# Attention and a long convolution on one core: early jobs in single PSUM banks, sums inverted as 128 rows of 32, and other due times for queries and output projection

## The chip, the core and the metric

The kernel runs on one core of one Trainium2 chip. The core has five engines with queues of their own: PE (matrix products, with PEld for its weight loads), DVE (vector), ACT (scalar functions), POOL, and SP, which here issues nearly all transfers. [...] PE writes its results to PSUM, which has eight banks of 512 fp32 columns on 128 partitions; DVE and ACT empty them to SBUF. The metric is the device time of one execution in microseconds.

## The reference

Two independent parts are computed and laid side by side along the last axis: attention with 32 query heads that share one key head and one value head of 16 columns, and a gated long convolution.

```python
q = (x @ wq).reshape(B, S, H, Dh).transpose(0, 2, 1, 3)      # S 2048, D 512, H 32, Dh 16
k, v = x @ wk, x @ wv
p = softmax(einsum("bhqd,bkd->bhqk", q, k) * Dh ** -0.5)
a = einsum("bhqk,bkd->bhqd", p, v).transpose(0, 2, 1, 3).reshape(B, S, H * Dh) @ wo
...
k_shift = sum(k_pad[:, t:t + S, :] * shift_k[:, ks - 1 - t] for t in range(4))
kv = k_shift * B_v
y = irfft(rfft(kv, 2 * S) * rfft(ssm_k, 2 * S))[:S] + kv * ssm_D
out = concatenate([a, B_q * y], axis=-1)
```

## The kernel before

**Turns and stacks.** The attention is cut into 16 stacks of 8 heads and 512 queries (`NST = 16`, stack n has token chunk n // 4 and head group n % 4). A stack has 64 turns, the whole 1024. A turn is one score tile of 128 x 1024 in two PSUM banks (`scores`, line 1206: eight products in tiles of 64 rows by 32 columns), one exponential of it on ACT (`exp`, 1227, the operation at line 1229) and half a product with the values (`pv`, 1235, 1259). The row that keeps the exponent in range and the row of ones in `vx`, from which each query's sum comes, go through the same products. The probabilities of the first eight turns are kept (`HELD = 8`), and their products with the values come late in stack 0. Each finished stack is copied out of PSUM (`acc_out`, 1273), written to DRAM (`od`), read again in another layout and divided by its sums (`heads`, 1341): two loads (`r`, the sums copied to the 16 rows of each head, and `o`), a clamp (1350), a reciprocal of 128 x 512 (1352), and three vector operations that make two fp16 halves `oc` of the quotient. The last stack is normalised in SBUF (`over`, 1452) in two halves.

**An order written out ahead.** The program is made by a planner in Python that keeps a clock for each of PE, ACT and DVE (`self.pe`, `self.act`, `self.dv`) and writes every engine's instructions in the order in which its own costs let them come; the chip runs this fixed order, whatever the real times. `attend` (1287) walks the turns. In a turn it writes the scores, then either a product with values or other work for PE, as long as its planned end is within a limit behind the turn's start T, then the exponential, one or two DMA issues, and what DVE has time for. Costs are in `T_EXP, T_SC, T_PV, LAT` and the like (47, 48); a DVE step states its cost with `yield`, as `yield T_REC` (700 ns) ahead of the reciprocal.

**Early jobs.** Before turn 64 the other work is a list of early jobs (`early_jobs`, 915): turning x of later token chunks (`turned`, `x_turn`), their keys and values (`keys`, `own`, `values`), the queries of head group 1, a bound, and two small products. Each writes one of the two halves of a single two-bank tile `F` and has vector steps that empty it. `early_fill` (1043) picks by due time, for as many units of 216 ns as fit within `EARLY_LIM = 480`. `kdone` and `vdone` are the times from which scores and products of a chunk of 512 keys may use it.

**Fill.** Later the other work is a list of jobs (`fill`, 238; the products at line 308), each with a due turn; of those whose inputs are there, the one with the least due turn is taken, one at a time, in the two-bank tile `f`. They are the convolution of two blocks of 256 channels, as transforms by products with tables (`short`, `long`, `backward`, due turns in `DUE`, line 45) with 16-point transforms and products of spectra on DVE between them (`dft16`, `product`), the queries of the remaining groups, two at a time (`q_group`, 1082; `rest_of_q`, 1133), and the output projection (`wo_job`, 1389; `wo_part`, 1396) for four stacks at a time. Line 467 empties a forward transform, 647 a last one, 1094 a query job, 1405, 1418 and 1435 projections.

**What waits for what around the change.** In `rest_of_q` a query group is begun at turn `due - 110` with `due = 256 c + 128 h - 40`, and its job is due 120 turns before `due`. `stacks` (1162) loads a stack's queries about 58 turns ahead. `heads(n)` for n from 4 on waits until the projection of the four stacks before (`("wo", n // 4 - 1)`) is done, as `oc` has four buffers. The projection of stacks 4c to 4c + 3 is due at turn `256 (c + 1) + 150`: 406, 662, 918. At the end, `last` (1473) writes what is left of the jobs, then the second half's `over`, the last product and the last store.

**Prologue.** Chunk 0 is turned, its keys and its group 0 queries are made in tile `acc`, the 512 columns of keys spread to 128 rows in `F[:, 0]` (`rows_mm`), and their maximum is spread by a product into `F[:, 1]` (880), from which the bound's weights `wbz` are made (883). All four transposes of chunk 1 are done here.

## Time and profile before

| | |
|---|---|
| three runs | 1032.59, 1037.88, 1040.52 us; median 1037.88 us |
| the profiled execution | 1034.93 us, of which its span is 1033.2 us |
| granted TensorE clock | 0.990 of full speed |
| first exponential begins, last one ends | 20.66 us, 1008.6 us |
| the costliest lines | exponential 947.9 us (ACT), values 553.1 us and scores 435.0 us (PE, overlapping), 50.3 us of reciprocals (DVE) |
| transfers | 84.86 MB, mean 82 GB/s |

Times in views are microseconds from the span's start. Busy time of an engine is the union of its instructions; matmuls are pipelined, so that a busy PE is not at its peak. Behind a group of instructions stands the idle time of its engine just before them, and what ended it.

### The profile page before, as it was taken

The page shows a single profiled execution, that of the slowest core. Times are in us where ns is not written, and L with a number is a line of the kernel's source. Part 1 is how long each engine was busy: PE and PEld are TensorE (multiplying, and loading weights), DVE is VectorE, ACT ScalarE, POOL GpSimd, SP SyncE. Part 2 cuts the span into 40 slices and gives each one's busy share as a digit, 9 for nine tenths or more (in the row PEclk, how much of TensorE's full clock was granted, in tenths as well). Part 3 has the DMA queues.
Part 4 walks back from the last instruction along what each step waited for, and adds up shares of the span by engine and source line. Part 5 has one row for each costly group of instructions (what it writes and reads, how often), then busy time and mean ns, then how long its engine had stood idle before and what let it go on. Part 6 is the DMA issues. An engine that isn't in the chain of part 4 may idle for free.

```text
span 1033.2 us, 53539 instructions
## 1 busy us (share of the span) xinstructions
PE 947.0 (92%) x24556; PEld 486.1 (47%) x24556; DVE 698.2 (68%) x827; ACT 963.0 (93%) x1035; POOL 42.9 (4%) x106
## 2 busy tenths in 40 slices
PE   7799999998999999889999999999899988889985
PEld 4334444544554554344545555555444433335661
DVE  4324488659963499999954994464949999980303
ACT  4699999999999999999999999999899999989880
POOL 3820000000000000000000000000000000000000
PEclk9899999999999999999999999999999999999997
DMA  6123354232112513101133352433220120103311
GB/s 217 42 97 117 114 154 136 70 115 65 49 54 85 151 24 100 34 27 55 34 110 93 103 151 95 137 101 90 80 81 23 48 55 3 59 5 99 119 35 55
DMA packets 78020, 84.86 MB, mean 82 GB/s; under 512 B 10734, under 2 KB 66392, under 8 KB 77788
## 3 DMA queue, kind: packets, MB, share of 16 engines
q1 hardware_dynamic: 76156, 80.77, 25.9%
q8 instruction: 194, 3.18, 1.3%
q10 hardware_dynamic: 1632, 0.60, 0.2%
q14 instruction: 38, 0.31, 0.1%
HBM read 55.91 MB, written 25.43 MB: 79 GB/s over the span
## 4 chain that ended last, share of the span: by engine, by line
ACT 42%; DVE 25%; PE 23%; issue 10%; DMA 0%; ACTq 0%; POOL 0%; DVEq 0%; POOLq 0%
ACT p L1229 41%; PE a L1259 9%; DVE sp L368 6%; PE s L1222 5%; PE f L308 5%; DVE r L1352 2%; DVE sp L437 2%; DVE u L411 1%; DVE sp L413 1%; DVE sp L415 1%; DVE t L437 1%; DVE sp L467 1%; PE s L720 1%; PE f L851 1%; PE f L727 1%
## 5 line engine op out<-in xcount | busy, mean ns | idle before, releaser
L1229 ACT ACTIVATE p<-s 128x1024 f32<-128x1024 f32 x1016 | 947.9, 1046 | 28.6 <-PE s L1222 25.5
L1259 PE MATMUL a<-p,vx 64*32 64x512 f32 (+1 forms) x8640 | 553.1, 565 | 1.1 <-issue 1.1
L1222 PE MATMUL s<-st,kst 49*32 49x512 f16 x8192 | 435.0, 380 | 47.1 <-ACT p L1229 42.0
L1222 PEld LDWEIGHTS <-kst 49*32 49x32 f16 x8192 | 199.7, 89 | 366.9 <-issue 325.9
L1259 PEld LDWEIGHTS a<-p,vx 64*32 64x32 f32 x8640 | 172.3, 106 | 26.8 <-issue 3.7
L368 DVE TENSOR_TENSOR sp<-sp 128x1024 f32<-128x1024 f32 x96 | 111.0, 1218 | 0.0
L467 DVE COPY sp<-f 128x1024 f32<-128x1024 f32 x32 | 39.1, 1223 | 85.9 <-PE f L308 85.8
L308 PE MATMUL f<-wo,o 64*32 64x512 f16 x1440 | 56.0, 379 | 4.2 <-DVE wp L1418 2.6
L368 DVE TENSOR_TENSOR sp<-sp,sp 128x1024 f32<-128x1024 f32 x48 | 56.2, 1220 | 0.4
L308 PE MATMUL f<-sp,fi 64*32 64x128 f32 (+1 forms) x1472 | 51.4, 312 | 3.1 <-issue 2.6
L308 PE MATMUL f<-xT,wq 64*32 64x512 f16 x1344 | 51.0, 375 | 1.8 <-DVE sp L467 1.6
L1352 DVE RECIPROCAL r<-r 128x512 f32<-128x512 f32 x15 | 50.3, 3353 | 0.5
L1275 DVE COPY ao<-a 128x1024 f32<-128x1024 f32 x15 | 18.4, 1225 | 46.0 <-PE a L1259 45.9
L279 POOL MEMSET tok<- 1x2 f32 x58 | 5.4, 93 | 936.0 <-PE f L308 928.3
L308 PE MATMUL f<-hT,ff 64*32 64x256 f32 (+1 forms) x1376 | 41.2, 321 | 2.1 <-DVE sp L467 1.8
L308 PE MATMUL f<-va,ff 64*32 64x128 f32 (+1 forms) x1504 | 41.6, 308 | 1.1 <-DVE va L555 1.1
L647 DVE TENSOR_TENSOR q<-f,q 128x1024 f32<-128x1024 f32 x8 | 9.8, 1225 | 47.2 <-PE f L308 47.2
L308 PEld LDWEIGHTS f<-sp,fi 64*32 64x32 f32 x1472 | 32.3, 105 | 15.4 <-issue 5.9
L308 PEld LDWEIGHTS f<-va,ff 64*32 64x32 f32 x1504 | 28.2, 106 | 16.0 <-issue 3.4
L552 DVE TENSOR_TENSOR va<-va,t 128x512 f32<-128x512 f32 x48 | 33.2, 691 | 1.4
L550 DVE TENSOR_TENSOR t<-kk 128x512 f32<-128x512 f32 x48 | 33.1, 689 | 1.0
L308 PEld LDWEIGHTS f<-hT,ff 64*32 64x32 f32 x1376 | 26.2, 106 | 15.8 <-issue 3.7
(162 smaller groups left out, 576.1 us busy)
## 6 DMA issues: line engine op xcount, KB each, us to landing
ff<-in_ff SPq DMA_DIRECT2D x64, 128.0 KB
od<-ao SPq DMA_DIRECT2D x30, 256.0 KB
qd<-qp SPq DMA_DIRECT2D x45, 128.0 KB
st<-qd SPq DMA_DIRECT2D x60, 96.0 KB
kk<-in_B_k SPq DMA_DIRECT2D x38, 128.0 KB
va<-in_B_v SPq DMA_DIRECT2D x32, 128.0 KB
hin<-in_B_ssm_k SPq DMA_DIRECT2D x32, 128.0 KB
fi<-in_fi SPq DMA_DIRECT2D x32, 128.0 KB
```

Of the source, the lines that this page charges most:

```text
L308: last = self.nc.tensor.matmul(F[32 * q : 32 * q + 32, rho, cols + a : cols + b], w[rows, 32 * q : 32 * q + 32], x[rows, a:b], start=begin ...
L368: v.tensor_tensor(part(out), part(a), part(b), op)
L411: v.tensor_scalar(u, x, float(np.sin(ang)), None, ALU.mult)
L437: self.nc.vector.tensor_tensor(out, a, b, op)
L467: self.nc.vector.tensor_copy(c[:, :, 2 * m2 : 2 * m2 + 2, :].rearrange("p q m n -> p m q n"), F.rearrange("p m (q n) -> p m q n", q=2))
L550: v.tensor_tensor(tmp, kx(i), tap(i), ALU.mult)
L552: v.tensor_tensor(a, a, tmp, ALU.add)
L1222: self.nc.tensor.matmul(out, self.kst[rows, c0 : c0 + 32], x, start=True, stop=True)
L1229: i = self.nc.scalar.activation(p, self.s, AF.Exp, scale=DH**-0.5 / SC / SC)
L1259: nc.tensor.matmul(out, self.vx[rows, k, :], p, start=i == 0, stop=i == NK - 1)
L1275: self.nc.vector.tensor_copy(a, self.acc)
L1352: nc.vector.reciprocal(r, r)
```

## The change

**Early jobs.** The two-bank tile `F` and its pool are gone in the early stage. A new pool `pb` has two tags of one bank each, and every early job gets a tile of its own in one of them (`one`); the pool of the fill's tile `f` is opened when the first fill job asks for it. Items of early jobs carry planned costs in ns instead of units: a transpose 440, a half of the keys 440, two products of 256 columns for the rows of keys (450 each) instead of four of 128, the values as four items of 230. A job is taken if it is ready within 150 ns, an item if it ends within `EARLY_LIM`, now 1000, of T, with `T_SHAPE` = 220 for the first item of a turn. Ties are broken by the order in the list. The early stage counts as over only when DVE has emptied the last job.

**Prologue.** One transpose of chunk 1 (dk 3) moves to the early jobs, with the split of weight groups 2 and 3 on POOL behind it. The product that spreads the maximum writes `pa[:, 1]`, and two transposes stand before it instead of one. The scaling of one of them goes from ACT to DVE.

**Sums.** For stacks 0 to 13 the sums are loaded as 128 rows of 32 (`rl`), clamped and inverted there, written to DRAM (`rd`) and loaded again, copied 16 times. Arrivals are planned at 8000 and 9000 ns after the issue, by a new argument of `fetch`. Stack 14 keeps the old layout, with the reciprocal cut in four quarters and `T_REC` = 860 for each.

**Due times.** A query group's `due` is 60 turns later for all groups but the first (`+ 20` for `- 40`; the first's is the same), and it is begun up to 500 turns ahead instead of 110. The projection's due turns become 400, 720 and 860.

```diff
-T_REC = 700.0
+T_REC = 860.0
+WO_DUE = (400, 720, 860)
-FILL_LIM, EARLY_LIM, PV_LIM, T_SWAP = 380.0, 480.0, 600.0, 1100.0
+FILL_LIM, EARLY_LIM, PV_LIM, T_SWAP, T_SHAPE = 380.0, 1000.0, 600.0, 1100.0, 220.0
...
+    def one(self, n):
+        return self.pb.tile([P, 512], F32, tag=f"b{n}", name=self.nm("b"))
...
-        c = slice(i * P, i * P + P)
-        self.nc.tensor.matmul(b[:, c], self.msk[:, PROJ], kvs[:, c], start=i == 0, stop=i == 3)
+        c = slice(i * 256, i * 256 + 256)
+        self.nc.tensor.matmul(b[:, c], self.msk[:, PROJ], kvs[:, c], start=i == 0, stop=i == 1)
...
-        self.x_turn(1, 0, acc[:, 0])
-        self.k_max(0, F[:, 0])
-        h16 = self.k_high(0, F[:, 0], nc.scalar)
-        self.k_rows(0, F[:, 0], h16)
-        nc.tensor.matmul(F[:, 1, 0:1], self.msk[:, REP], self.kmx[:, 0:1], start=True, stop=True)
+        self.k_max(0, rows)
+        h16 = self.k_high(0, rows, nc.scalar)
+        self.k_rows(0, rows, h16)
+        self.x_turn(1, 0, pa[:, 0])
+        x1 = self.one(1)
+        self.x_turn(1, 1, x1)
+        nc.tensor.matmul(pa[:, 1, 0:1], self.msk[:, REP], self.kmx[:, 0:1], start=True, stop=True)
...
-    def early_fill(self, units, force=False):
+    def early_fill(self, limit, force=False):
         began = False
-        while units > 0:
-            ready = lambda j: max([s.t for s in j[2]] + [min(b.t for b in self.bank)])
-            new = [j for j in self.early if ready(j) < INF and (force or ready(j) + LAT <= self.pe + (units - 1) * T_UNIT)]
+        end = lambda cost: self.pe + cost + (0.0 if began else T_SHAPE) <= limit
+        while True:
+            ready = lambda j: max([s.t for s in j[2]] + [min(b.t for b in self.bank)]) + LAT
+            new = [j for j in self.early if ready(j) < INF and (force or max(self.pe, ready(j)) - self.pe < 150.0)]
...
-                due = 4 * 64 * c + 128 * h - (40 if c or h else -40)
-                yield lambda now: self.turn >= due - 110
+                due = 256 * c + 128 * h + (20 if c or h else 40)
+                yield lambda now: self.turn >= due - 500
...
-        h = self.fetch([(r, od[DH:32]), (o, od[0:DH])], self.od_h[n], first=True)
-        yield self.at(h)
-        yield 400.0
-        nc.vector.tensor_scalar(r, r, 1e-30, 1 / OS, ALU.max, ALU.mult)
-        yield T_REC
-        nc.vector.reciprocal(r, r)
+        if n < NST - 2:
+            rl = w.tile([P, 32], F32, tag="rl", bufs=2, name=self.nm("rl"))
+            h = self.fetch([(rl, od[DH].rearrange("h (a b) -> h a b", b=32))], self.od_h[n], first=True, arrive=8000.0)
+            h1 = self.fetch([(o, od[0:DH])], self.od_h[n], first=True, arrive=9000.0)
+            yield self.at(h)
+            yield 120.0
+            nc.vector.tensor_scalar(rl, rl, 1e-30, 1 / OS, ALU.max, ALU.mult)
+            yield 300.0
+            nc.vector.reciprocal(rl, rl)
+            rd = self.rd[n].rearrange("(i h) n -> i h n", i=1)
+            h = self.fetch([(self.rd[n].rearrange("h (a b) -> h a b", b=32), rl)], Stamp(self.dv), first=True)
+            h = self.fetch([(r, rd.broadcast_to([DH, 8, 512]))], h, first=True, arrive=9000.0)
+            yield self.at(h, h1)
+        else:
+            h = self.fetch([(r, od[DH:32]), (o, od[0:DH])], self.od_h[n], first=True)
+            yield self.at(h)
+            yield 430.0
+            nc.vector.tensor_scalar(r, r, 1e-30, 1 / OS, ALU.max, ALU.mult)
+            for i in range(4):
+                yield T_REC
+                nc.vector.reciprocal(r[:, i * P : (i + 1) * P], r[:, i * P : (i + 1) * P])
...
-                j = self.wo_job(i, range(4 * c, 4 * c + 4), out, 256 * (c + 1) + 150)
+                j = self.wo_job(i, range(4 * c, 4 * c + 4), out, WO_DUE[c])
```

147 lines of the change are left out of this document (76 added, 71 removed).

## The prediction, made before the changed kernel ran

> **What bounds the kernel now.** I read the page first, then a table of the span cut at its stages, then what ACT and PE waited for, then the DVE and PE order at the places where ACT waited.
>
> ```profile
> span 1033.2 us, 53539 instructions
> PE 947.0 (92%) x24556; PEld 486.1 (47%) x24556; DVE 698.2 (68%) x827; ACT 963.0 (93%) x1035; POOL 42.9 (4%) x106
> L1229 ACT ACTIVATE p<-s 128x1024 f32<-128x1024 f32 x1016 | 947.9, 1046 | 28.6 <-PE s L1222 25.5
> ```
>
> These three lines are of the page: the span, busy time by engine, and the costliest group, with what ended ACT's idle time. The table by stage:
>
> ```profile
> 20.66:45.34 24.68, 18.22 (x241) 9.11 (x234) 9.57 (x22) 15.74 (x16) 23.45 (x24) 0.86 0.15 44
> 45.34:84.00 38.66, 36.93 (x692) 14.90 (x696) 14.98 (x32) 35.23 (x36) 8.39 (x10) 1.00 0.24 78
> 84.00:395.00 311.00, 297.58 (x7868) 151.31 (x7854) 214.09 (x250) 308.88 (x333) 1.88 (x21) 1.00 0.32 93
> 395.00:525.00 130.00, 118.64 (x2924) 57.97 (x2909) 123.46 (x128) 127.23 (x138) 0.62 (x7) 1.00 0.18 53
> 525.00:770.00 245.00, 237.60 (x6776) 127.87 (x6767) 152.59 (x177) 241.87 (x262) 2.42 (x20) 1.00 0.35 103
> 770.00:927.00 157.00, 135.52 (x3224) 60.92 (x3223) 150.04 (x172) 151.62 (x165) 1.49 (x6) 0.99 0.13 38
> 958.50:1008.60 50.10, 45.03 (x1679) 33.42 (x1686) 10.23 (x10) 43.64 (x46) 0.36 (x4) 1.00 0.23 71
> 1008.60:1033.20 24.60, 12.25 (x165) 3.84 (x147) 9.67 (x22) 0.03 (x1) 0.09 (x1) 0.78 0.14 52
> ```
>
> The table's columns are the stretch, its length, then busy time of PE, PEld, DVE, ACT and POOL with counts, and the granted clock. ACT's exponentials, one per turn, set the time: 333 of them in the 311 us from 84 to 395, 0.934 us each, with ACT busy 308.88. PE and DVE count only where they make ACT wait, and that is in four places. First, the early stage: 52 exponentials in 63.3 us, so 63.3 - 52 x 0.934 = 14.8 us too many. Second, the long middle from 84 to 927: ACT idle is 2.1 + 2.8 + 3.1 + 5.4 = 13.4 us, 8.2 of it in the two stretches (395 to 525, 770 to 927) where DVE is busy 95% and PE is not full. Third, the last stack: 46 in 50.1 us, 7.1 us over. Fourth, 24.6 us after the last exponential, in which ACT does nothing.
>
> **The change part by part.** All sums are against this execution: 1034.9 us with what lies around its 1033.2 us span. It is 3 us under the median of the three runs, 1037.9; they reach from 1032.6 to 1040.5.
>
> *Prologue.*
>
> ```profile
> 17.39 0.38 PE L880 MATMUL f<-kmx,msk 128*128 128x1 f32 x2 [1.44 <-DVE kst L789]
> ```
>
> The product that spreads the key maximum waited 1.44 us for a vector instruction that reads the other bank of the same tile; in the new order it writes a tile that this instruction does not read, behind two transposes instead of one. What follows it (the copy kmr, wbz, the products with it, the first scores) comes earlier by at most 1.44 minus the second transpose, about 0.7 us, and by nothing if the copy still stands behind L789 on DVE. One copy goes from ACT to DVE and one transposition into the early jobs; both are behind the first scores. The first 128x512 projection in two products of 256 columns instead of four of 128 streams the same columns: 0. I take -0.7 (0 to -1).
>
> *Early jobs.* Two edits pull against each other.
>
> ```profile
> PE f L768 <- DVE kmx L792: 1.6, 2, 0.8
> PE f L740 <- DVE xc L931: 1.2, 1, 1.2
> PE f L727 <- DVE vx L775: 1.2, 1, 1.2
> PE f L764 <- DVE xf L931: 1.1, 1, 1.1
> ```
>
> The waits of PE are given as total, times and longest. Two rows of the table by stage, and ACT's order, where the bracket is the idle time before:
>
> ```profile
> 30.00:32.60 2.60, 1.67 (x33) 1.05 (x31) 1.71 (x3) 1.84 (x3) 2.43 (x3) 1.00 0.53 154
> 32.60:39.40 6.80, 5.40 (x56) 2.11 (x48) 2.56 (x7) 3.53 (x4) 6.47 (x6) 0.50 0.14 42
> ```
>
> ```profile
> 35.62 1.02 ACT L1229 ACTIVATE p<-s 128x1024 f32<-128x1024 f32 x1 [1.54 <-PE s L1222]
> 37.52 1.02 ACT L1229 ACTIVATE p<-s 128x1024 f32<-128x1024 f32 x1 [0.88 <-PE s L1222]
> 39.65 1.94 ACT L1229 ACTIVATE p<-s 128x1024 f32<-128x1024 f32 x2 [1.10 <-PE s L1222]
> ```
>
> Each wait of PE here (5.1 us in four rows) stands in PE's queue in front of the next scores, and most are for an instruction that empties the other bank. With a tile for each bank, and a rule that a job begins only when it is ready within 150 ns of planned time, most of the 5.1 us goes. The dip of the granted clock to 0.50 from 32.6 to 39.4 adds three gaps, 3.5 us. On the other side, EARLY_LIM goes from 480 to 1000: a job may end 1000 ns after the turn's planned start T, the next scores take 216 and the latency 60, so the next exponential starts at T + 1276 instead of T + 904 at worst, 0.37 us late in each turn with a job. The 22 early jobs of the list, the longer ones spread over several turns, make some 30 turns with a job, so 11 us at worst, less the 220 ns of changing shape for each group that disappears when jobs are put together. So the ends are -11 (waits, dip and half of the changes of shape gone) and +6 (11 lost, 5 won). I take -6, nearer the gain, because PE is busy only 18.22 of 24.68 us in the first stretch, where most of the loss is: there is room to do the same work without making ACT late.
>
> [...]
>
> POOL gets the last two weight splits behind one more split of x. It is busy 23.45 of 24.68 us there, but their reader, the queries of the remaining groups, starts only when the early jobs are over: 0. Those jobs now also count as open until DVE has emptied them: under 1 us, where fill work is plentiful: 0.
>
> *A stack's sums as 128 rows of 32.*
>
> ```profile
> L1352 DVE RECIPROCAL r<-r 128x512 f32<-128x512 f32 x15 | 50.3, 3353 | 0.5
> L1350 DVE TENSOR_SCALAR r<-r 128x512 f32<-128x512 f32 x15 | 6.3, 421 | 16.9 <-DMA r<-od 16.9
> 1018.38 0.18 DVE L1462 TENSOR_SCALAR lr<-lr 128x16 f32<-128x16 f32 x1
> 1018.59 0.26 DVE L1464 RECIPROCAL lr<-lr 128x16 f32<-128x16 f32 x1
> ```
>
> And two places in ACT's order:
>
> ```profile
> 744.58 57.53 ACT L1229 ACTIVATE p<-s 128x1024 f32<-128x1024 f32 x62 [1.56 <-PE s L1222]
> 915.55 1.02 ACT L1229 ACTIVATE p<-s 128x1024 f32<-128x1024 f32 x1 [3.48 <-PE s L1222]
> ```
>
> A reciprocal of 512 columns takes 3353 ns and one of 16 takes 260, so 32 take about 360, and the clamp about 180: 14 stacks save 14 x (3353 + 421 - 540) = 45 us of DVE. The planner booked 700 ns for each reciprocal, so DVE fell 2.65 us behind the written order at every one, and whatever it had to empty next came late to PE, then to ACT. The gaps at 744.58 and 915.55 each follow one or two reciprocals. Stack 14 keeps its way, cut in four quarters of about 840 ns, now booked 860. Each of the 14 stacks issues two more transfers on SP (the inverted rows out, their copies back), 28 in all at 0.55 us; SP is mostly waiting, so 0, unless the load of the copies stands waiting for the store just ahead of it, with the loads of the next scores behind it. DVE also waited 16.9 us for these loads before; the planned arrival goes from 6000 to 8000 and 9000 ns, so less is left. Value in the middle: between -11 (all but the 2 us of the first stretch) and +4 (new waits for the three transfers). I take -6, half of the 13.4 us, as the two stretches with DVE at 95% are where the work goes.
>
> *Queries sooner, output projection moved.* This sets the end.
>
> ```profile
> 656.02 1.23 DVE L1094 TENSOR_SCALAR qp<-f 128x1024 f16<-128x1024 f32 x1 [8.56 <-PE f L308]
> 711.25 1.23 DVE L1405 TENSOR_SCALAR wp<-f 128x1024 f32<-128x1024 f32 x1 [7.24 <-PE f L308]
> 761.36 1.22 DVE L1094 TENSOR_SCALAR qp<-f 128x1024 f16<-128x1024 f32 x1
> 769.99 1.23 DVE L467 COPY sp<-f 128x1024 f32<-128x1024 f32 x1 [5.03 <-PE f L308]
> ```
>
> Those rows are of the time ahead of the second block's transforms. At the end stand:
>
> ```profile
> 1002.60 1.23 DVE L647 TENSOR_TENSOR q<-f,q 128x1024 f32<-128x1024 f32 x1 [13.65 <-PE f L308]
> 1007.88 2.70 PE L1259 MATMUL a<-p,vx 64*32 64x256 f32 x80
> 1008.14 1.23 DVE L1435 SCALAR_TENSOR_TENSOR wp<-f,wp 128x1024 f32<-128x1024 f32 x1 [4.32 <-PE f L308]
> 1017.57 0.77 DVE L1459 STREAM_TRANSPOSE lr<-a 128x256 f32<-128x256 f32 x2
> ```
>
> The second block's convolution waits for its last forward transform, emptied at 769.99. Just ahead of it PE's fill went to two query jobs (656.02, 761.36) and an output projection (711.25), each some 9 to 19 us of the small room that PE has beside scores and values. With the start of the queries 370 turns sooner and their due times 60 turns later, these jobs fall into 395 to 525, where PE is busy 118.64 of 130 us and the convolution waits for DVE; the projection, due at 720 instead of 662, stands behind the forward transforms. Two query jobs and a projection at 10 to 19 us make 30 to 57 us by which 769.99 comes sooner, and three reciprocals fewer take 10 us off the DVE stretch to 927. Against it, three query groups add some 20 us of DVE work to 395 to 525, and the saved reciprocals there give back 10. So the inverse transforms can begin 30 to 45 us sooner, and their last product need not be emptied at 1002.60, in the last stack. Their eight loads and the 24 moved loads of x go with them on SP: 0. What that is worth: of the 7.1 us of the last stack -4 (0 to -7), since the projections of stacks 12 to 14 stay there. In the tail the last values end at 1007.88 + 2.70 = 1010.58, but the final normalisation starts at 1017.57, behind the projection emptied at 1008.14 and one more job: -6.5 (0 to -7).
>
> Sum: -0.7 - 6 - 6 - 4 - 6.5 = -23, so 1012 beside the profiled execution and **1015** beside the median.
>
> **The rivals.**
>
> *The dip stays.* The clock fell after a stretch in which PE was busy 1.67 of 2.60 us, 64%; a new order that leaves PE as idle in the first 20 us brings the dip back, 3.5 us of the early gain are not had, and 1018.5 comes out. Against it: jobs put together leave fewer short idles. [...]
>
> *The gaps are exchanged.* ACT pays 0.37 us in most early turns (+5 instead of -6), and late transfers take the place of late reciprocals in the middle (0 instead of -6); only the end is shorter: 1015 + 17 = 1032. For it: PE is busy 36.93 of 38.66 us from 45 to 84. Against it: the middle gaps follow the reciprocals.
>
> *The chain of stacks is late (slower).* Stacks 8 to 11 are normalised only when the projection of 4 to 7 is done, 12 and 13 only after that of 8 to 11, 14 after 13.
>
> ```profile
> 953.42 0.55 SPq L170 DMA_DIRECT2D r<-od  x1
> 956.79 0.43 DVE L1350 TENSOR_SCALAR r<-r 128x512 f32<-128x512 f32 x1 [4.50 <-DMA r<-od]
> ```
>
> One transfer took 3.4 us here; a stack now has three in a row, 10 us by this row and 23 us by the planner's arrival times (8 + 6 + 9), which decide, as DVE's order follows them. With issue and vector work that is 28 us for each. If the projection of 4 to 7 ends near 765 instead of 711 (due 58 turns later), stacks 8 to 11 are ready at 877, and their projection stands behind the inverse transforms to about 945; then stacks 12 and 13 take 57, stack 14 10 and the last jobs with the tail 35 us: 1047 in the span, 1052 with the rest. It decides from about 930, where before is reached.
>
> *More than the sum.* DVE is nowhere late, and early stage, middle and last stack lose a third of what they lose now: -10 - 9 - 5 - 7 - 0.7 = -32, 1006.
>
> *It does not do what it says.* The order of fill work hardly moves, as every query job waits for x in one buffer, and the banks still wait for each other: only the reciprocals count: 1032.
>
> **How the numbers follow.** A measurement of this kernel tells about 1% from no change, 1027.5 to 1048. Chances: forecast 0.42, dip stays 0.10, more 0.14, gaps exchanged 0.18, does not do it 0.06, chain late 0.10. The likeliest alone runs from 1006 to 1026. Faster takes the forecast, the dip, more and some 0.04 of the exchanged gaps: 0.70. Slower takes 0.06 of the late chain. The same is 0.24. The range goes from 998, below the better case by the prologue's and the middle's bounds, to 1035, above the exchanged gaps; the late chain and a still larger gain are left out.
>
> **What would show it.** Right: 52 early exponentials in under 58 us; no PE wait on DVE across banks; ACT idle under 8 us between 84 and 927; the convolution's last transform emptied before 740 and its last output before 960; the final transpose within 1 us of the last values. Wrong: more 0.3 us gaps before the exponentials of the first 50 turns, DVE waiting for the copies of the inverted rows, or the projection of stacks 8 to 11 emptied after 900.

## The result, and the profile after

| | median | runs | ratio to before, with its 95% interval |
|---|---|---|---|
| before | 1039.2 us | 4 runs, 1032.59 to 1041.31 | 1 |
| changed | 1005.77 us | 4 runs, 1004.52 to 1007.34 | 0.969 [0.9642, 0.9737] |

The changed kernel is 3.1% faster. The forecast was 2.2% (1015 beside a median of 1037.9), and 1005.77 lies in its range of 998 to 1035. The profiled execution of the changed kernel took 1007.34 us. The page of its profile begins:

```profile
span 1005.6 us, 53610 instructions
PE 947.9 (94%) x24556; PEld 483.1 (48%) x24556; DVE 652.6 (65%) x831; ACT 960.8 (96%) x1034; POOL 43.2 (4%) x106
L1244 ACT ACTIVATE p<-s 128x1024 f32<-128x1024 f32 x1016 | 946.1, 1046 | 12.9 <-PE s L1237 8.1
```

The work is the same but for DVE, which has 45.6 us less (652.6 for 698.2). The exponentials are as busy as before (946.1 for 947.9), and the idle time ahead of them has shrunk from 28.6 to 12.9 us. So the gain is waiting, of ACT inside the turns and of everything behind the last turn. The table by stage, with the columns of the earlier one (stretch, length, busy PE, PEld, DVE, ACT, POOL, granted clock, DMA share, GB/s):

```profile
19.24:43.34 24.10, 22.59 (x236) 11.32 (x231) 8.85 (x21) 15.61 (x16) 22.87 (x23) 0.59 0.16 45
43.34:82.00 38.66, 38.53 (x708) 15.76 (x702) 16.86 (x36) 36.03 (x38) 10.27 (x12) 1.00 0.26 85
82.00:395.00 313.00, 304.10 (x8172) 155.46 (x8171) 224.38 (x271) 311.13 (x335) 2.19 (x22) 1.00 0.34 98
395.00:525.00 130.00, 123.93 (x3220) 63.25 (x3205) 109.20 (x122) 128.75 (x139) 1.04 (x10) 1.00 0.26 74
525.00:770.00 245.00, 231.32 (x6244) 116.96 (x6236) 171.97 (x231) 244.41 (x265) 2.08 (x16) 1.00 0.31 91
770.00:927.00 157.00, 144.41 (x3816) 72.64 (x3808) 90.23 (x104) 155.90 (x170) 0.54 (x6) 1.00 0.20 61
929.50:990.00 60.50, 58.22 (x1952) 35.75 (x1951) 17.03 (x24) 59.56 (x65) 1.39 (x7) 1.00 0.13 39
990.00:1005.60 15.60, 6.53 (x80) 2.14 (x64) 4.57 (x11) 0.00 (x0) 0.00 (x0) 0.76 0.11 39
```

From 82 to 927 ACT is idle 1.87 + 1.25 + 0.59 + 1.10 = 4.8 us, where it was idle 13.4 us from 84 to 927. In the stretches 395 to 525 and 770 to 927 DVE was busy 95% and is now busy 84% and 57%. Behind the last exponential lie 15.6 us, where there were 24.6. But the first row shows no gain: 16 exponentials in 24.10 us (24.68 before), now at a granted clock of 0.59 (0.86 before).

The waits of PE (total, times, longest) name no vector instruction that empties the other bank of a shared tile:

```profile
PE s L1237 <- ACT p L1244: 36.1, 106, 0.5
PE s L728 <- DVE lr L1500: 2.9, 1, 2.9
PE s L1237 <- ACT held L1244: 1.4, 2, 0.7
PE f L606 <- DVE sp L475: 1.3, 2, 0.8
PE b L858 <- DVE tok L834: 1.2, 1, 1.2
PE s L900 <- DVE wbz L893: 1.0, 1, 1.0
```

The waits on `p` are the normal pace of the scores. The four rows of waits for `kmx`, `xc`, `vx` and `xf` are gone. The end, in the order of DVE and PE (start, duration, instruction, in brackets the idle time before):

```profile
661.78 0.35 DVE L1369 RECIPROCAL rl<-rl 128x32 f32<-128x32 f32 x1
714.16 1.23 DVE L475 COPY sp<-f 128x1024 f32<-128x1024 f32 x1 [4.68 <-PE f L316]
924.17 1.22 DVE L655 TENSOR_TENSOR q<-f,q 128x1024 f32<-128x1024 f32 x1 [13.00 <-PE f L316]
981.19 1.23 DVE L1475 TENSOR_TENSOR y<-f,wp 128x1024 f32<-128x1024 f32 x1 [13.73 <-PE f L316]
988.40 2.79 PE L1274 MATMUL a<-p,vx 64*32 64x256 f32 x96
991.31 0.78 DVE L1488 STREAM_TRANSPOSE lr<-a 128x256 f32<-128x256 f32 x2 [8.90 <-PE a L1274]
994.14 5.34 PE L728 MATMUL s<-wl,lr 128*32 128x512 f32 x32 [2.95 <-DVE lr L1500]
```

The last forward transform is emptied at 714.16 (769.99 before), the last product of the convolution at 924.17 (1002.60). The last projection ahead of the tail is emptied at 981.19, so DVE stands idle 8.90 us until the last values end at 988.40 + 2.79 = 991.19, and the final transpose follows 0.12 us later.

All later statements on stages go by one table. It is made from the start of the 1st, 17th, 65th and 961st exponential, the end of the last, and the end of the span, in the profiled execution of each kernel (us):

| kernel | first exponential | turns 0-15 | 16-63 | 64-959 | 960 to last | tail | early time at low clock |
|---|---|---|---|---|---|---|---|
| before | 20.7 | 24.7 | 50.6 | 845.2 | 67.5 | 24.5 | 6.8 |
| changed | 19.2 | 24.1 | 50.0 | 836.2 | 60.4 | 15.6 | 20.5 |
| changed, profiled again | 19.9 | 21.6 | 50.0 | 837.0 | 61.2 | 15.9 | 13.7 |
| old early jobs | 21.6 | 29.9 | 50.6 | 831.9 | 63.3 | 19.1 | 27.3 |
| old sums | 18.8 | 20.4 | 50.0 | 847.9 | 60.6 | 16.6 | 10.2 |
| old sums, booked | 19.3 | 21.3 | 50.0 | 835.7 | 67.6 | 21.9 | 13.7 |
| old queries | 19.1 | 24.0 | 50.0 | 835.3 | 65.8 | 21.5 | 20.5 |
| old projection | 19.3 | 24.3 | 50.0 | 836.7 | 62.1 | 14.6 | 20.5 |
| before, booked | 21.5 | 28.6 | 50.6 | 833.8 | 70.6 | 34.8 | 23.9 |
| warm | 19.2 | 20.1 | 50.0 | 835.5 | 61.5 | 15.6 | 0 |
| old early jobs, warm | 21.3 | 24.1 | 50.6 | 833.1 | 63.0 | 19.6 | 0 |
| warm, one tile | 23.5 | 23.7 | 53.1 | 836.2 | 60.3 | 15.3 | 6.8 |
| warm, limit 480 | 20.1 | 19.0 | 64.1 | 834.7 | 65.1 | 19.6 | 6.8 |
| warm tail | 20.0 | 20.1 | 50.0 | 835.6 | 60.6 | 14.7 | 0 |

The spans of the two profiled executions differ by 27.6 us: 1.4 in the prologue, 1.2 in the first 64 turns, 8.9 in the middle, 7.1 in the last stack, 8.9 in the tail. The last column is a warning about this comparison: it gives the time at half clock before turn 64 (in two rows, before booked and warm with one tile, the sum of two dips), and the two executions had dips of different length, 6.8 and 20.5 us.

### The profile page after: what moved, and what is told of

Its sections match the earlier page's. It is cut to its first block, busy times and chain, and to the rows that moved or that the text cites. A ratio compares the mean times of both kernels' runs of the same rounds, so it can differ in the third digit from the quotient of the medians.

```text
span 1005.6 us, 53610 instructions
## 1 busy us (share of the span) xinstructions
PE 947.9 (94%) x24556; PEld 483.1 (48%) x24556; DVE 652.6 (65%) x831; ACT 960.8 (96%) x1034; POOL 43.2 (4%) x106
## 4 chain that ended last, share of the span: by engine, by line
ACT 68%; issue 14%; PE 14%; DVE 3%; DMA 1%; ACTq 0%; SPq 0%; DVEq 0%
ACT p L1244 67%; PE a L1274 5%; PE s L1237 4%; PE f L316 1%; DMA xc<-in_A_x 1%; PE b L735 1%; DMA wkvf<-in_A_wv 1%; DVE u L419 1%; DVE sp L421 1%; PE s L728 1%; PE b L775 1%; DVE sp L475 0%; PE b L772 0%; DVE sp L423 0%; PE b L748 0%
## 5 line engine op out<-in xcount | busy, mean ns | idle before, releaser
L1244 ACT ACTIVATE p<-s 128x1024 f32<-128x1024 f32 x1016 | 946.1, 1046 | 12.9 <-PE s L1237 8.1
L1237 PE MATMUL s<-st,kst 49*32 49x512 f16 x8192 | 428.8, 383 | 43.5 <-ACT p L1244 36.1
L1274 PEld LDWEIGHTS a<-p,vx 64*32 64x32 f32 x8640 | 168.0, 106 | 24.6 <-issue 2.8
L475 DVE COPY sp<-f 128x1024 f32<-128x1024 f32 x32 | 39.2, 1224 | 87.8 <-PE f L316 87.6
L316 PE MATMUL f<-sp,fi 64*32 64x128 f32 (+1 forms) x1424 | 40.3, 315 | 0.0
L316 PEld LDWEIGHTS f<-va,ff 64*32 64x32 f32 x1472 | 26.8, 106 | 15.3 <-issue 3.3
L316 PEld LDWEIGHTS f<-sp,fi 64*32 64x32 f32 x1424 | 26.4, 106 | 10.2 <-issue 3.0
L316 PEld LDWEIGHTS <-o 64*32 64x32 f16 x1440 | 23.2, 93 | 15.7 <-issue 4.2
```

The source lines that it names most:

```text
L316: last = self.nc.tensor.matmul(F[32 * q : 32 * q + 32, rho, cols + a : cols + b], w[rows, 32 * q : 32 * q + 32], x[rows, a:b], start=begin ...
L475: self.nc.vector.tensor_copy(c[:, :, 2 * m2 : 2 * m2 + 2, :].rearrange("p q m n -> p m q n"), F.rearrange("p m (q n) -> p m q n", q=2))
L1237: self.nc.tensor.matmul(out, self.kst[rows, c0 : c0 + 32], x, start=True, stop=True)
L1244: i = self.nc.scalar.activation(p, self.s, AF.Exp, scale=DH**-0.5 / SC / SC)
L1274: nc.tensor.matmul(out, self.vx[rows, k, :], p, start=i == 0, stop=i == NK - 1)
```

## The experiments

Three sets of kernels ran, each set on a chip of its own and with its own runs of before, whose medians are 1040.1, 1040.2 and 1040.5 us. Times are compared across the sets on the strength of that. Times are medians, with the range of the runs, and the ratio to before with its interval. A difference that is called the price of a part is the difference of two medians; the runs of one kernel spread over some 2 to 11 us.

### One part undone at a time

**Early jobs and prologue of before** (no_early), all else as changed. The second hunk stands for the whole: prologue, list of early jobs and `early_fill` are those of before.

```diff
-FILL_LIM, EARLY_LIM, PV_LIM, T_SWAP, T_SHAPE = 380.0, 1000.0, 600.0, 1100.0, 220.0
+FILL_LIM, EARLY_LIM, PV_LIM, T_SWAP = 380.0, 480.0, 600.0, 1100.0
...
-        pa, b = self.wide("pa"), [self.one(i) for i in range(2)]
+        acc, F = self.wide("pa"), self.wide("pf")
```

> The changed kernel without its first part: prologue and early jobs are as before (two-bank tile, limit 480), sums, due times of queries and projection as changed. Theory: the two traces differ by 1.4 us at the first exponential and by 1.2 us in the next 63 turns, so that this part is worth about 3 us and the time is about 1009 (1007 to 1011); the gaps from turn 64 on and the tail stay as in the changed kernel. Rival: the long dip of the granted clock is peculiar to the profiled execution, and the early jobs save the 6 us that were forecast: 1013 or more.

Measured: 1013.21 us (1011.67 to 1018.79), 0.9741 [0.9715, 0.9767]. The early part is worth some 7.3 us beside the changed kernel's 1005.89 below, more than the 1.2 us by which the first 64 turns of the two traces differ. The theory (1007 to 1011) missed; the rival's 1013 or more came, barely. The runs of this kernel fall apart by the granted clock: three with a mean of 0.994 took 1011.67 to 1012.12 us, one with 0.992 took 1014.3, two with 0.983 and 0.985 took 1018.25 and 1018.79. The profiled one is of the last kind. The stretch of its dip:

```profile
19.20:46.60 27.40, 23.75 (x204) 12.22 (x205) 10.39 (x22) 13.95 (x15) 25.48 (x25) 0.50 0.14 40
```

**The sums' old way** (old_sums): `heads` and `T_REC` = 700 as before.

```diff
-T_REC = 860.0
+T_REC = 700.0
...
-        if n < NST - 2:
-            rl = w.tile([P, 32], F32, tag="rl", bufs=2, name=self.nm("rl"))
...
+        yield T_REC
+        nc.vector.reciprocal(r, r)
```

> The changed kernel with all 15 stacks inverted as 128 x 512 and 700 ns booked for it, as before. Theory: DVE lags 2.65 us behind the written order at each reciprocal again, ACT's idle time between turns 64 and 960 grows by about 8 us, and 45 us more DVE work pushes the last transforms later, so that some 5 us of the end are lost too: 1015 to 1022. Rival: the due times alone made the middle and the end: 1008 or less.

Measured: 1017.65 us (1016.06 to 1019.1), 0.9782 [0.9761, 0.9803], so 11.8 us over the changed kernel. The middle takes 847.9 us instead of 837.0, which is nearly all of it; last stack and tail (60.6 + 16.6) are close to those of the changed kernel (61.2 + 15.9), so the theory's total came, but not the 5 us that it looked for at the end. One place in its trace, in the orders of DVE and ACT:

```profile
468.95 3.35 DVE L1366 RECIPROCAL r<-r 128x512 f32<-128x512 f32 x1
477.24 1.22 DVE L475 COPY sp<-f 128x1024 f32<-128x1024 f32 x1
480.19 1.02 ACT L1244 ACTIVATE p<-s 128x1024 f32<-128x1024 f32 x1 [2.75 <-PE s L1237]
```

Behind the long reciprocal DVE works without a pause until it empties a transform, and ACT is then idle 2.75 us ahead of an exponential that the scores release.

**The queries' old due times** (old_queries).

```diff
-                due = 256 * c + 128 * h + (20 if c or h else 40)
-                yield lambda now: self.turn >= due - 500
+                due = 4 * 64 * c + 128 * h - (40 if c or h else -40)
+                yield lambda now: self.turn >= due - 110
```

> The changed kernel with the queries' due turns and start of before (40 turns earlier due instead of 20 later, begun 110 turns ahead instead of 500). Theory: the last forward transform of the second block is emptied some 30 us later (744 instead of 714), the last inverse one near 955 instead of 924, and 3 to 8 us of last stack and tail come back: 1009 to 1014. Rival: the time saved on DVE keeps the end free in any case: 1006 to 1008.

Measured: 1014.67 us (1013.18 to 1017.45), 0.9746 [0.9726, 0.9767], 8.8 us over the changed kernel. Last stack and tail take 65.8 + 21.5 us instead of 61.2 + 15.9. In the order of DVE:

```profile
730.12 1.23 DVE L475 COPY sp<-f 128x1024 f32<-128x1024 f32 x1 [5.70 <-PE f L316]
957.94 1.23 DVE L655 TENSOR_TENSOR q<-f,q 128x1024 f32<-128x1024 f32 x1 [6.06 <-PE f L316]
1000.28 1.23 DVE L1475 TENSOR_TENSOR y<-f,wp 128x1024 f32<-128x1024 f32 x1 [3.72 <-PE f L316]
1001.42 0.77 DVE L1488 STREAM_TRANSPOSE lr<-a 128x256 f32<-128x256 f32 x2
```

The last forward transform is 16 us later than in the changed kernel, where 30 were expected, and the convolution's last output 34 us. With them the last projection moves behind the last exponential, which ends at 994.19: the final transpose stands behind the projection emptied at 1000.28.

**The projection's old due times** (old_projection), with the changed kernel once more beside it (changed_again).

```diff
-WO_DUE = (400, 720, 860)
+WO_DUE = (406, 662, 918)
```

> The changed kernel with the projection's due turns of before (406, 662, 918). If the parts simply add up, 6 us are left for this one after 7, 12 and 9 for the others: 1010 to 1013, with the projection of stacks 4 to 7 ahead of the second block's last forward transforms again. Rival: the due turns hardly matter, as the projection is done when PE has room: 1005 to 1008.

> The changed kernel as it is, as the measure for the runs beside it: 1004 to 1008, with a dip of the early clock whose length is a whole number of steps of 3.41 us.

Measured: 1005.32 us (1003.09 to 1010.41), 0.9662 [0.9638, 0.9686], beside 1005.89 (1005.56 to 1010.05), 0.9674 [0.9652, 0.9695] for the changed kernel. The due times do nothing. In the two traces DVE, ACT and POOL execute the same instructions in the same order, and the transfers are issued in the same order, so that this run is nearly a repetition of the changed kernel. The second job of the projection of stacks 4 to 7 is emptied at the same time; first with the old due times, then as changed:

```profile
651.73 1.23 DVE L1434 TENSOR_SCALAR wp<-f 128x1024 f32<-128x1024 f32 x1 [9.47 <-PE f L316]
```

```profile
649.91 1.22 DVE L1434 TENSOR_SCALAR wp<-f 128x1024 f32<-128x1024 f32 x1 [9.47 <-PE f L316]
```

A due time only decides between jobs that are ready together, and here both lead to the same order. The job moved from 711 to 650 us all the same, with the rest of the change.

The parts undone cost 7.3 + 11.8 + 8.8 - 0.6 = 27.3 us, against 1040.2 - 1005.9 = 34.3 us for all of them. The other 7 us do not belong to one part alone; as pairs of parts were not undone together, where they come from is not shown.

### Is it the length of the reciprocal, or that the plan had it wrong?

**Before, with the reciprocal booked at its real length** (booked). Not an instruction is removed; only the order changes.

```diff
-T_REC = 700.0
+T_REC = 3350.0
```

> The kernel before with one constant changed: 3350 ns booked for each reciprocal instead of 700, its length on the chip. No DVE time is saved. Theory of the lag (a step that the planner does not know of makes the next ones late): ACT's idle time between turns 64 and 960 shrinks by about 6 us, some of the end comes back too: 1028 to 1034. Rival (the 45 us of DVE time are what counts): 1037 to 1042, as the kernel before.

Measured: 1038.77 us (1032.08 to 1041.79, 12 runs), 0.9973 [0.9951, 0.9996]. By the total the booking does almost nothing. By stages it does two large things. Here are its middle, last stack and tail:

```profile
100.80:934.60 833.80, 785.91 (x20688) 397.04 (x20673) 635.80 (x720) 830.96 (x897) 6.54 (x54) 1.00 0.27 79
934.60:1005.20 70.60, 62.59 (x2194) 44.73 (x2201) 13.22 (x12) 60.81 (x65) 0.36 (x4) 0.98 0.28 86
1005.20:1040.00 34.80, 17.28 (x288) 5.71 (x270) 11.34 (x23) 0.04 (x1) 0.27 (x3) 0.88 0.14 49
```

and the middle of before, from the same exponential to the same:

```profile
95.97:941.13 845.16, 789.20 (x20736) 397.89 (x20728) 636.39 (x720) 831.97 (x898) 6.42 (x54) 1.00 0.27 80
```

The middle falls by 11.4 us, to 833.8, with the same 636 us of DVE. So what made ACT wait there was the wrong booking. But the plan now leaves 2.65 us more of DVE at each stack, so the chain of the convolution comes later against the exponentials: its last output stands 5.6 us behind the end of the last exponential (1005.24), where in before it stood 6.0 us ahead of it (1002.60 and 1008.63):

```profile
1010.88 1.22 DVE L647 TENSOR_TENSOR q<-f,q 128x1024 f32<-128x1024 f32 x1 [11.94 <-PE f L308]
```

Last stack and tail take 3.1 and 10.3 us more, and the gain is gone. So the theory of the lag has its mechanism confirmed and its total (1028 to 1034) missed; the rival gives the total. (The first 16 turns are 4.0 us longer in this execution, whose early dips are 23.9 us long against 6.8.)

**The same in the changed kernel** (old_sums_booked): the sums' old way with 3350 booked.

```diff
-T_REC = 860.0
+T_REC = 3350.0
...
+        yield T_REC
+        nc.vector.reciprocal(r, r)
```

> The changed kernel with all 15 stacks inverted as 128 x 512, and 3350 ns booked for it. Beside old_sums (1017.7, 700 booked) and the changed kernel (1005.9) it tells the lag from the DVE time. Theory of the lag: the middle is as short as in the changed kernel, the end perhaps 1 to 4 us longer: 1006 to 1011. Rival: the 45 us of DVE time are worth 5 us or more by themselves: 1011 to 1017.

Measured: 1015.74 us (1013.24 to 1017.48), 0.975 [0.9728, 0.9772], not told apart from the old sums booked at 700 (1017.65), and in the range of the rival. The middle is free of the waits (835.7 us, the changed kernel 837.0), and the end pays (67.6 + 21.9 instead of 61.2 + 15.9):

```profile
976.36 1.22 DVE L655 TENSOR_TENSOR q<-f,q 128x1024 f32<-128x1024 f32 x1 [11.30 <-PE f L316]
999.10 1.23 DVE L1460 TENSOR_TENSOR y<-f,wp 128x1024 f32<-128x1024 f32 x1 [6.66 <-PE f L316]
```

So 45 us of DVE cost 10 to 12 us in the changed kernel whichever way they are planned: as waits of ACT in the middle when booked too short, as a chain some 50 us later (976 instead of 924) when booked right. The change removes the time itself, and neither is paid.

### The dip of the clock

**Dummy products to keep PE busy** (warm). Copies of small products, whose results are never read, go into the prologue and into the turns 1 to 11.

```diff
+        for i in range(12):
+            r = slice(32 * (i % 4), 32 * (i % 4) + 32)
+            nc.tensor.matmul(put[i % 4 // 2][:, i % 2], self.sel[r, 0], qp[r, 0], start=True, stop=True)
...
+        for i in range(3):
+            nc.tensor.matmul(pa[:, i % 2], self.sel[:, 0], qp[:, 0], start=True, stop=True)
...
+        if 1 <= t < 12:
+            for i in range(2):
+                self.nc.tensor.matmul(self.pa0[:, i], self.sel[:, 0], self.kst[:, 0:512], start=True, stop=True)
```

> The changed kernel with products added that only keep PE busy: 15 in the prologue's waits, and two after the scores of turns 1 to 11, into the two banks that the values use later; their results are never read. Theory: the dip of the granted clock from 18.7 to 39 us (PE instructions at half speed for 20 us) is what ate the early gain, and comes from PE's short idles; it goes or shrinks to a few us, the first 16 exponentials take 16 to 20 us instead of 24.1, and the time is 1000 to 1003. Rival: the clock falls whatever PE does, or the products stand in the way of the scores: 1006 or more.

Measured: 1003.62 us (1002.42 to 1003.99), 0.9641 [0.9621, 0.9661]. The dip is gone: the granted clock is 1.00 throughout the first 16 turns, which take 20.07 us. The time lies 0.6 us above the range of the theory and 2.4 below the rival's. Here are, of this kernel, the 3.4 us that end where the clock falls in the changed one, and the first 16 turns:

```profile
15.50:18.90 3.40, 3.06 (x41) 1.38 (x41) 2.29 (x6) 2.62 (x5) 0.00 (x0) 1.00 0.94 261
19.22:39.29 20.07, 19.59 (x258) 9.68 (x254) 9.41 (x21) 15.59 (x16) 18.30 (x17) 1.00 0.21 57
```

and of the changed kernel, ahead of the fall and in the dip:

```profile
15.10:18.50 3.40, 1.88 (x19) 1.00 (x19) 2.08 (x5) 2.83 (x5) 0.04 (x1) 1.00 1.11 322
18.50:39.20 20.70, 19.22 (x169) 9.74 (x169) 8.30 (x20) 11.86 (x12) 19.71 (x18) 0.51 0.21 56
```

PE is busy 3.06 of 3.40 us with the dummies, 1.88 of 3.40 us without. In the dip PE is busy 19.22 of 20.70 us with 169 products, 8.2 in a us; at full clock the first 16 turns hold 258, of which 22 are dummies, so 236 in 20.07 us or 11.8 in a us. In the dip the scores themselves are late: one of their products took 606 ns there and 386 ns from 40 to 59 us (medians of 104 and 152), and from 18.5 to 39.2 us ACT stood idle 7.7 us ahead of exponentials that the scores released.

**The same with the old early jobs** (no_early_warm): 20 dummy products ahead of the product that spreads the maximum, and two in each of the turns 1 to 11.

```diff
+        put = [self.wide() for _ in range(2)]
+        for i in range(20):
+            r = slice(32 * (i % 4), 32 * (i % 4) + 32)
+            nc.tensor.matmul(put[i % 4 // 2][:, i % 2], self.sel[r, 0], qp[r, 0], start=True, stop=True)
```

> The run without the early part, with the same kind of added products that keep PE busy (20 ahead of the product that spreads the maximum, two after the scores of turns 1 to 11; results never read). Beside the run warm (1003.6) it prices the early part without the dip. Theory: a prologue later by 1.4 us and PE's waits across the two banks are left, 1006 to 1010. Rival: all that the early part brought was a shorter dip, 1003 to 1005.

Measured: 1014.17 us (1013.12 to 1014.79), 0.9744 [0.9727, 0.9761]. This is 10.5 us over warm, with no dip in either, and above both theory and rival: the price of the old early part, with dummies in both. Its stages against those of warm: prologue + 2.1, first 16 turns + 4.0, to turn 63 + 0.6, middle - 2.4, last stack + 1.5, tail + 4.0.

```profile
21.32:45.37 24.05, 21.70 (x263) 9.88 (x256) 10.07 (x22) 15.87 (x16) 22.83 (x24) 1.00 0.15 45
```

```profile
995.26 1.22 DVE L1469 TENSOR_TENSOR y<-f,wp 128x1024 f32<-128x1024 f32 x1 [13.23 <-PE f L309]
996.40 0.77 DVE L1482 STREAM_TRANSPOSE lr<-a 128x256 f32<-128x256 f32 x2
```

So the early part reaches to the end. The fill's first query products come in turn 62 instead of 58, the last forward transform is emptied at 730.17 instead of warm's 710.24, the convolution's last output at 954.01 instead of 919.40, and one projection is left standing ahead of the final transpose. Against expectation, the total is no better than the median of no_early (1013.21): it lies 4 us below its runs with a clock of 0.983 and 0.985 and 2 us above those with 0.994. So the dummies seem to cost some 2 us here, and the 10.5 us may be too much by that; the price of the old early part lies between 7 and 10.5 us.

**Dummy products behind the last values** (warm_tail), on top of warm.

```diff
+        for i in range(13):
+            nc.tensor.matmul(s[:, i % 2], self.sel[:, 0], self.kst[:, 0:512], start=True, stop=True)
```

> The run warm with 13 more products after the last values, while PE waits 3 us for the final normalisation; results never read. Theory: the granted clock falls in that wait, and the last 32 products take 5.3 us where full clock would take some 3.5; with the clock kept the tail is 1.5 us shorter: 1001.5 to 1002.8. Rival: the tail's products are not bound by the clock: 1003.6.

Measured: 1003.04 us (1002.64 to 1004.38), 0.9641 [0.962, 0.9661], not told apart from warm by the total. The last 32 products do get shorter, 3.64 us instead of warm's 5.34, at a granted clock of 1.00 instead of 0.68, and the tail of the trace is 0.9 us shorter (14.7 for 15.6), where 1.5 were expected; first this kernel, then warm:

```profile
990.24 3.64 PE L728 MATMUL s<-wl,lr 128*32 128x512 f32 x32
```

```profile
990.41 5.34 PE L728 MATMUL s<-wl,lr 128*32 128x512 f32 x32 [2.95 <-DVE lr L1509]
```

### What in the early part does it

**Both banks as halves of one tile again** (warm_one_tile), in the new order, on top of warm.

```diff
     def one(self, n):
-        return self.pb.tile([P, 512], F32, tag=f"b{n}", name=self.nm("b"))
+        if not hasattr(self, "two"):
+            self.two = self.pb.tile([P, 2, 512], F32, tag="b", name="two")
+        return self.two[:, n]
```

> The run warm (1003.6, no dip) with one change: all early jobs write the two halves of one two-bank tile again, as before. Prices the single-bank tiles alone. Theory: PE's waits for the vector instruction on the other bank come back, 5 us in PE's queue, of which 2 to 5 us reach ACT: 1006 to 1009. Rival: what counts in the early part is the planner's new limits and costs, 1003 to 1005.

Measured: 1013.81 us (1011.74 to 1014.61), 0.9734 [0.9712, 0.9756], 10.2 us over warm, about twice the most that was expected. Against warm: prologue + 4.2, first 16 turns + 3.6, the next 48 + 3.1, the later stages within 1.2 us of warm's. Two dips of the clock of 3.4 us are back too, the first behind the longest wait, so a part of the first two figures may be the clock's. The waits across the banks are back in the list of waits of PE:

```profile
PE two L737 <- DVE kst L798: 3.2, 1, 3.2
PE two L777 <- DVE kmx L801: 3.0, 3, 1.3
PE two L774 <- DVE xf L946: 1.1, 1, 1.1
```

The order was planned as if the banks were free of each other, which may be why the shared tile costs more here than the 5.1 us of waits seen in before; its price in the order of before was not measured. Of the prologue's 4.2 us, 3.2 are the wait of one transpose of chunk 1 for the vector instruction that makes the keys (`kst`) out of the other half.

**The old limit of an early job** (warm_lim480), on top of warm.

```diff
-FILL_LIM, EARLY_LIM, PV_LIM, T_SWAP, T_SHAPE = 380.0, 1000.0, 600.0, 1100.0, 220.0
+FILL_LIM, EARLY_LIM, PV_LIM, T_SWAP, T_SHAPE = 380.0, 480.0, 600.0, 1100.0, 220.0
```

> The run warm with EARLY_LIM 480 instead of 1000. Theory (the forecast's trade): a limit of 1000 lets jobs push exponentials by up to 0.37 us in a turn, so that 480 gives fewer such gaps in the first 64 turns, but ends the early jobs some turns later, which comes back as a later convolution: 1002 to 1007. Rival: the wide limit is what frees the early stage, 1008 or more.

Measured: 1023.91 us (1021.84 to 1024.99), 0.983 [0.9808, 0.9853], 20.3 us over warm. The rival came. The first 16 turns are 1.1 us shorter than warm's, so the larger limit does cost a little there. But the jobs come too slowly: the keys of chunk 3 are not there at turn 48, and ACT stands still for 11 us ahead of this turn's exponential, while `attend` writes the missing jobs first:

```profile
83.39 2.12 ACT L1253 ACTIVATE p<-s 128x1024 f32<-128x1024 f32 x2 [11.01 <-PE s L1243]
```

The turns 16 to 63 take 14.1 us more. The rest is at the end, which goes with the fill's later start (last stack + 3.6, tail + 4.0).

## Why the prediction was right, and where it was not

**What bounds the kernel.** Right: but for 1.4 us of the prologue the time went from the four places named (early stage, gaps of the middle, last stack, tail), and the exponential's own 0.93 us a turn did not move. The forecast of 1015 stands 9 us above the measured 1005.8. In the profiled executions 27.6 us went where 23 were forecast, which is half of this. The other half goes with the dip: the profiled execution of before lies some 5 us below the median of the later runs, with a short dip, and that of the changed kernel had a long one. The counts in the forecast's readings are of all ACT instructions, so that 333 and 46 exponentials are really 332 and 45; the sums move by under 1 us.

**Prologue, -0.7 (0 to -1).** The first exponential came 1.4 us sooner (20.66 to 19.24); over all traces without dummies it begins at 20.7 to 21.6 us with the old prologue and at 18.8 to 19.9 with the new one. The bound of -1 was too narrow, because a second wait across banks was left out. Before, the copy of the first keys waited until the query products in the other half of `acc` were done; with the queries in a tile of their own it follows the key products. First before, then changed:

```profile
13.20 0.58 ACT L868 COPY kvs<-a 128x512 f32<-128x512 f32 x1 [3.09 <-PE a L720]
```

```profile
12.14 0.59 ACT L876 COPY kvs<-a 128x512 f32<-128x512 f32 x1 [2.23 <-PE a L741]
```

Counted from the copies of x ahead of it (8.17 and 7.98), this is 0.9 us. The wait that the forecast named is gone as well, but there its own proviso came true: the copy `kmr` now stands directly behind the vector instruction for the keys, and from the copy of the keys to `kmr` only 0.3 us were won.

**Early jobs, -6 (-11 to +6).** The value was near what the part was worth in the runs (7.3 us, 10.5 with dummies in both), but not where it was looked for, and the two traces alone show next to nothing: 1.2 us in the first 64 turns. That the number is near is partly luck, since some of it is won at the end. The sign that was named, 52 exponentials in under 58 us, did not come: they take 62.6 us (63.7 before), and 58.6 even in warm, without a dip. The step that failed is "most of the 5.1 us goes. The dip ... adds three gaps, 3.5 us", which took the dip as something that the change would end; that ending these waits ends it without dummies, no run shows (with dummies, warm_one_tile has the waits and 6.8 us of dips, warm neither). The waits did go, and ending them was worth some 10 us in this order, counting what the shared tile does to the clock (warm_one_tile). The dip stayed and was longer in this execution (20.5 us of low clock for 6.8), which hid the gain in the traces. The upper end, + 6 for a limit of 1000, was the wrong fear: the limit costs 1 us in the first 16 turns and at 480 the changed order loses 20. What the sum left out is that the early part also moves the convolution: with the old one the last forward transform is 20 us later (no_early_warm).

The rival "the dip stays" was thus true in that the dip stayed, and its time (1018.5) wrong, because the other terms were larger than taken. Its reason, that a stretch with PE busy 64% brings the dip, does not hold: before itself kept its clock behind a stretch busy 58% (last section). Nor did a long wait of PE bring it: in the changed kernel none ahead of the fall was longer than 1.2 us, and PE was busy 1.88 of the 3.40 us before it.

**Sums as 128 rows of 32, -6 (-11 to +4).** The durations were right: 0.35 us for the reciprocal (360 ns forecast), DVE busy time down by 45.6 us (45 forecast); only the quarters of stack 14 take 910 ns instead of 840. The size was off: 11.8 us when undone, nearly all in the middle, past the bound of -11. The mechanism, "DVE fell 2.65 us behind the written order at every one", is shown by booked, where 11.4 us leave the middle without an instruction removed. But it is not the whole: booked right, the same DVE time is paid at the end. "Half of the 13.4 us" was mis-sized: by the booking alone, ACT's idle time in the middle falls from 845.16 - 831.97 = 13.2 to 833.80 - 830.96 = 2.8 us. Of the signs of being wrong, DVE waiting for the copies of the inverted rows came once, 7.4 us ahead of 902 us; ACT, idle 1.1 us in the whole of 770 to 927, did not feel it.

**Queries sooner.** Right in its direction, mis-sized in its parts. The last forward transform came 56 us sooner (forecast 30 to 57) and the convolution's last output 78 us, but undoing the queries alone moves them back by 16 and 34 us only, and undoing the early part (in the kernels with dummies) by 20 and 35 us. So the step that gave all of the 30 to 57 us to "Two query jobs and a projection" failed: the early part does as much, and the projection nothing. That the total fits is luck. Undoing the queries gives back 8.8 us, all at the end. "Last stack -4, tail -6.5" was too little: -7.1 and -8.9 in the traces, just outside the bound of -7 in the last stack and 1.9 outside it in the tail. The shares of the early part and of the reciprocals in the same chain were left out of this sum: the early part moves the tail by 4.0 us.

**Projection moved.** The step "the projection, due at 720 instead of 662, stands behind the forward transforms" failed: the projection of stacks 4 to 7 is emptied at 650, ahead of the last forward transform (714), and its due time has no effect (old_projection). The rival of a late chain rested on this step and fell with it: the projection of stacks 8 to 11 is emptied at 807 and 827 us, against 801 and 822 before and the 900 that would have shown it wrong.

**The other signs.** No PE wait across banks: came. ACT idle under 8 us from 84 to 927: 4.8. Last transform before 740 and last output before 960: 714 and 924. Final transpose within 1 us of the last values: 0.12 us. Of the signs of being wrong, short gaps (0.2 to 0.5 us) ahead of the first 50 exponentials are 3, where there was 1; the copies of the inverted rows and the projection stand above. Of the rivals, "more than the sum" with 1006 gives the time measured, but by another split than its own: it asked for 10 us in the early stage and 7 in the tail, and the traces show 1.2 and 8.9. Its time was met by luck.

## What to carry to other kernels

In an order that is written out ahead, a step booked too short makes others wait and a step booked right still has to be paid in the place where the chain is tight; only removing the time removes both. Give each PSUM bank that two engines use at once a tile of its own (worth 10.2 us in warm_one_tile), and plan the order for it. The two go together: the new order with the shared tile (1013.8) is no better than the old early part as a whole (1014.2), and the new tiles with the old limit (1023.9) are worse. Where the clock dips by a different length in each execution (here 20.5 and 13.7 us in two of one kernel), compare kernels with one part undone by the times of their runs, since two profiles may show two different dips.

The fastest kernels here are the changed one with the dummy products, 1003.62 us, 0.9641 [0.9621, 0.9661] of before, and the same with more of them in the tail (1003.04), beside 0.9674 [0.9652, 0.9695] for the changed kernel: some 2 us, with intervals that overlap.

## What the runs showed of the hardware

**Early in the span the clock fell without a PE gap of more than 1.0 us in the 3.4 us ahead, and the busy share of PE did not tell when.** In the changed kernel it fell at about 18.5 us, behind 3.4 us in which PE was busy 55% and waited at most 1.0 us at a time. In before it fell at 32.6, and the longest wait in the 3.4 us ahead was 0.9 us. Here are three of the five stretches of 3.41 us ahead of that:

```profile
15.53:18.94 3.41, 1.97 (x22) 1.04 (x20) 1.43 (x4) 2.29 (x4) 0.26 (x1) 1.00 1.03 277
22.36:25.77 3.41, 2.22 (x40) 1.15 (x39) 1.58 (x5) 2.18 (x3) 3.25 (x5) 1.00 0.00 0
29.19:32.60 3.41, 2.48 (x44) 1.75 (x36) 1.71 (x3) 2.40 (x3) 3.24 (x3) 1.00 0.60 181
```

PE is busy 58%, 65% and 73% in them, and the clock falls behind the last, the busiest. So in this trace no bound on this share, as the profile gives it, tells the stretch ahead of the fall from the others. What the dummies show is that in warm, with more for PE to do (busy 90% in the same place), there was no early dip, nor was there one in no_early_warm; with the same dummies, warm_one_tile and warm_lim480 had 6.8 us of it. What decides behind a stretch with short idles, no run here shows. Later in before, at 913.1 us, a dip of 3.4 us followed a wait of PE of 2.65 us, which began at 910.9. The lengths of the single dips ahead of the tail are 3.4 (that one), 6.8 (before), 10.2 (old sums), 13.7 (old sums, booked), 20.5 (changed) and 27.3 us (old early jobs), multiples of 3.41, an eighth of the longest, within 0.1 us.

**The same program has dips of different length.** Two profiled executions of the changed kernel had 20.5 and 13.7 us of low clock ahead of turn 64. The runs of before go with it: of 16 beside the second set, the fastest, 1032.43 us, had a mean granted clock of 0.993, the next, 1036.08, one of 0.992, and the others, from 1038.75 to 1043.66, had 0.980 to 0.987. The profiled execution of before, with 0.990, was among those with a short dip, some 5 us below the median of the later runs.
